# Window attention and a gated expert layer on one core: a visit's values moved ahead of its scores, and operand sums spread over 48 steps

## The chip, the cores and the metric

The kernel runs on one core of a Trainium2 chip. The metric is device time in microseconds (us) from start to end of one execution. Three executions of the kernel before took 1054.36, 1054.43 and 1058.17 us; the median is 1054.43. TensorE is called PE here, its weight loads PEld, VectorE DVE, ScalarE ACT, GpSimd POOL, and the DMA queue of SyncE SP.

## The reference

```python
# q, k, v: (8 batches, 8 heads, 576 positions, 64)
scores = q @ k^T / 8, masked to the 64 positions up to the query's own
attn   = softmax(scores) @ v
x      = attn as (4608 tokens, 512)
xn     = x / sqrt(mean(x*x) + 1e-6) * rms_g
out    = (silu(xn @ w_gate) * (xn @ w_val)) @ w_out     # 512 -> 1536 -> 512
```

## The kernel before

**Tiles and steps.** The 4608 tokens are nine tiles of 512 (t = 0 to 8). A tile's expert layer is 32 steps: 24 steps produce the 1536 hidden values (`expert_in`, from tile 3 on `expert_in_7`), 8 produce the output (`expert_out`); up to tile 2 both accumulate in the three banks of the pool `ps_mo`. Each step begins with `tick()`, which calls `advance` (L1105): it takes from a list called `plan`, sorted by step number, every piece of work whose step has come. Step 0 is the first of tile 0, step 32 the first of tile 1, and so on. From tile 1, chunk 3 (step 44) on, `group()` (L63) puts each group of PE instructions behind the PE instruction that was traced last before it, so PE runs the groups in the order of the program. Inside a group, and on ACT, DVE, POOL and SP, a list scheduler with a timeline of its own chooses the order before the kernel runs; each engine then executes its list in that fixed order and waits at its head.

**Attention.** Batches 2 to 7 are handled pair of heads by pair of heads, numbered n = 8 to 31, in visits. Visit n stands at step `visit_at(n)` (L613): 27, 32, 37, 42.5, 47.5, and then every 8 steps, so in a tile from the third on visits fall at steps 7.5, 15.5, 23.5 and 31.5. A visit (L618) computes the scores of pair n (`scores_of_pair`, L404) and the attention values of pair n-2 (`attention_values`, L498). The scores of blocks 1 to 8 go to two banks of PSUM named `sc` (32 small matmuls), those of block 0 to the last columns of a third bank (4 small matmuls, called `x` in the trace). The values' first part (g = 0, 20 matmuls) goes to the first 320 columns of this same bank `x`, the second part (g = 1, 16 matmuls) to a bank `xp`. Both come from the pool `ps_x`, which has two banks. DVE masks the scores block by block (L399, block 0 first), ACT takes exponentials (L402), DVE reciprocals (L428); POOL multiplies and moves the weights (`move`, L371, 16 instructions for a pair), DVE transposes them (`turn`, L374), and two visits later PE multiplies them with v. ACT copies the values out of the two banks (L564), squares them (L570); the squares are added up over the pairs (L575, POOL or DVE).

**Normalising.** At steps 25 and 27 of a tile the batch's sums of squares become roots (matmul `tot`, L700, into a bank of `ps_x`; then DVE L688 to L695), DVE scales x (L740), and from tile 3 on `combine` (L762) forms sums and differences on DVE (L779, L780, L782, L785) and casts them on ACT (L773) and POOL (L774).

**Operand sums.** From tile 3 on the hidden layer uses seven products of half-size blocks in place of eight. The sums of weights that this needs are made by `prepare` (L856), 24 pieces: for each of six chunks c, four steps. A piece is 8, 4, 4 or 8 PE matmuls with a signed unit matrix into one bank called `chain` (pool `ps_mi`, one bank), a cast on ACT (L890, tile `hl`), a subtraction on DVE (L891) that reads the same bank, and two DMAs to DRAM (L893). The next piece writes the same bank, so its first matmul waits for the subtraction. The pieces stand at step `PREP0 + (PREP1 - PREP0) * j / 24`, j = 0 to 23.

Of the kernel before, what the change touches and what calls it, by code (L numbers as in the profile page):

```python
# [26 lines left out]
B, H, S, D = 8, 8, 576, 64  # L27
# [9 lines left out]
XSPLIT = 320  # L37
# [5 lines left out]
MOVES = (8.7, 7, 4.5, 4)  # L43
FIRST7 = 3
ORDERED = (1, 3)
PREP0, PREP1 = 32.2, 55.5
ST = 2 * NBLK * P - D
NRB = 2
S1, LK1, LV1, LQ1 = [-2, 1, 3, 6, 10, 12.5, 15.5, 19], 2.5, 6, 7
# [7 lines left out]
def tile_window_attention_moe(  # L57
# [34 lines left out]
    def x_bank(name):  # L92
        return ps_x.tile([P, TT], F32, tag="xp", name=name)
# [262 lines left out]
    def big(n):  # L356

        t = wk.tile([P, ST], I32, tag="st8", name=f"pm_{n}", bufs=NST).bitcast(F32)
        return (t[:, a : a + NBLK * P].rearrange("p (j k) -> p j k", k=P) for a in (0, ST - NBLK * P))

    def slot(u):

        return (u - 1) % NBLK
# [15 lines left out]
    def units(g, h):  # L379
        return [1 + 4 * g + 2 * h + i for i in range(2)] + ([0] if g == h == 0 else [])  # L380

    def quarter(out, qt, kk, h, j):

        halves = kk.rearrange("p (n c) -> p n c", c=D)
        hd = slice(h * D, (h + 1) * D)
        nc.tensor.matmul(  # L386
            out.rearrange("p (n c) -> p n c", c=D),
            lhsT=qt[hd, j * D : (j + 1) * D],
            rhs=halves[hd, :1, :] if j == 0 else halves[hd, j : j - 2 : -1, :] if j % 2 == 0 else halves[hd, j - 1 : j + 1, :],
            start=True,  # L390
            stop=True,
            skip_group_check=True,
        )
# [3 lines left out]
    def masked(out, sc, mask, low):  # L397

        nc.vector.tensor_tensor_reduce(out, sc, mask, -QK_SCALE, 3.0e38, ALU.add, ALU.min, low)  # L399

    def weigh(part, low, total):
        nc.scalar.activation(part, part, AF.Exp, bias=low, scale=-1.0, accum_out=total)  # L402

    def scores_of_pair(n, qk, first):  # L404

        qt, kk = qk
        sc = [
            pool.tile([P, TT], F32, tag=tag, name=f"sc_{n}_{h}").rearrange("p (i k) -> p i k", k=P)
            for h, (pool, tag) in enumerate(((ps_sc, "sc"), (ps_tr, "tr")))
        ]  # L410
        for h in range(2):
            quarter(first[h * D : (h + 1) * D, :D], qt, kk, h, 0)
        for i in range(4):
            for h, par in QUARTERS:
                quarter(sc[h][par * D : (par + 1) * D, i, :], qt, kk, h, 2 * i + 1 + par)
        p, m = big(n)
        st = wk.tile([P, 3, NBLK], F32, tag="st", name=f"st_{n}", bufs=3)
        order = [0] + [u for h in range(2) for u in units(0, h) + units(1, h) if u]
        place = {u: sc[h][:, 2 * g + i, :] for g in range(2) for h in range(2) for i, u in enumerate(units(g, h)) if u}
        for u in order:  # L420
            w, v = P if u else D, slot(u)
            masked(p[:, v, :w], place[u] if u else first[:, :D], blocked[:, :P] if u else blocked[:, P:],
                   st[:, 0, v : v + 1])
        for u in order:
            w, v = P if u else D, slot(u)
            weigh(p[:, v, :w], st[:, 0, v : v + 1], st[:, 1, v : v + 1])
        nc.vector.tensor_scalar(st[:, 1, :], st[:, 1, :], 1e-9, None, ALU.add)
        nc.vector.reciprocal(st[:, 2, :], st[:, 1, :])  # L428
        whole[n] = p, m, st[:, 2, :]
# [87 lines left out]
    def attention(b):  # L517
# [12 lines left out]
        def score(hp, g, first=None):  # L530
            qk = qs[hp], pairs[hp][0]
            if b < TB:
                soft[hp, g] = scores(b * NPAIR + hp, g, qk)
            elif g == 0:
                scores_of_pair(b * NPAIR + hp, qk, first)
# [75 lines left out]
    visits = {}  # L611
# [4 lines left out]
        return VISITS[n] if n < 4 else VISITS[4] + 8 * (n - 4)  # L616

    def visit(n):  # L618

        xp = x_bank(f"x0_{n}")  # L620
        if n in visits:
            visits[n][0](xp[:, XSPLIT:])
        if n - 2 in visits:
            visits[n - 2][1](0, xp)
            visits[n - 2][1](1)

    def first_batch():
        load_queries, load_keys, score, to_keys, values, roots, normal, moved, turned = attention(0)
# [430 lines left out]
    for n in range(NPAIR * TB, NPAIR * B + 2):  # L1059
        at_step(visit_at(n), partial(visit, n))  # L1060
# [117 lines left out]
```

## Time and profile before

| what | value |
|---|---|
| median of three executions | 1054.43 us |
| profiled execution | 1057.74 us, span of its instructions 1056.0 us |
| PE busy | 987.1 us (93%) |
| DVE, POOL, ACT busy | 626.5, 520.6, 510.0 us |
| granted clock of PE, mean of the span | 0.976 |

The span is from the first instruction's start to the last one's end. "Busy" is the union of an engine's instructions. A wait row names the instruction that stood at the head of its engine's queue and the instruction whose end released it. [...]

### The profile page before, as it was taken

To read this page: it belongs to the slowest core of one execution; us is meant where nothing else is said; L and a number is where in the kernel's file an instruction comes from. 1 tells how busy PE (TensorE), PEld (TensorE's weight loads), DVE (VectorE), ACT (ScalarE), POOL (GpSimd) and SP (SyncE) were. 2 spreads that over 40 slices of the span, in tenths; PEclk is the share of its full clock that TensorE was granted. 3 is DMA by queue.
4 is the path that set the end of the run, shared out by engine and by line. 5 is a ranking of instruction groups with operands and counts; after the bars stand their busy time and mean duration, and the time that the engine had idled before them with its cause. 6 is when DMAs were issued, how large, how long until landed. Compare 5 with 4: busy or idle time off the path is not lost.

```text
span 1056.0 us, 20885 instructions
## 1 busy us (share of the span) xinstructions
PE 987.1 (93%) x7883; PEld 645.8 (61%) x7895; DVE 626.5 (59%) x1655; ACT 510.0 (48%) x1303; POOL 520.6 (49%) x667
## 2 busy tenths in 40 slices
PE   7789987998899999989998999999989999999998
PEld 5544544454454445468846884688458847856875
DVE  5688857424457434856695669566856574531550
ACT  5557867235342434246535663565356524522531
POOL 3325635808256666756766575657575314200210
PEclk9889988999899999999999999899999999999999
DMA  7647853024231334147724672376235605632501
GB/s 282 196 155 217 263 174 91 31 62 139 72 114 56 115 116 136 64 123 231 219 69 141 216 216 68 116 231 212 72 102 180 180 33 144 206 110 83 157 2 40
DMA packets 81317, 143.45 MB, mean 136 GB/s; under 512 B 25792, under 2 KB 38336, under 8 KB 81216
## 3 DMA queue, kind: packets, MB, share of 16 engines
q1 hardware_dynamic: 80640, 140.93, 43.5%
q8 instruction: 62, 1.02, 0.4%
q10 hardware_dynamic: 576, 1.18, 0.3%
q14 instruction: 39, 0.32, 0.1%
HBM read 121.64 MB, written 20.45 MB: 135 GB/s over the span
## 4 chain that ended last, share of the span: by engine, by line
PE 53%; DVE 19%; POOL 13%; ACT 9%; issue 3%; DMA 2%; SPq 0%; DVEq 0%; POOLq 0%; ACTq 0%
PE bk L922 19%; POOL pm L371 12%; ACT pm L402 4%; PE bk L790 3%; PE bk L791 3%; PE bk L792 3%; DVE xb L740 3%; PE pv L790 2%; PE pg L790 2%; PE pv L792 2%; PE pg L791 2%; PE pv L791 2%; PE pg L792 2%; PE sc L386 2%; DVE pm L374 2%
## 5 line engine op out<-in xcount | busy, mean ns | idle before, releaser
L922 PEld LDWEIGHTS <-wt 128*128 128x128 f16 x3024 | 294.8, 98 | 48.1 <-issue 12.2
L371 POOL TENSOR_TENSOR pm<-pm,st 32x288 f32<-32x288 f32 (+1 forms) x384 | 262.8, 684 | 99.2 <-DVE st L428 38.6
L922 PE MATMUL bk<-xn,wt 128*128 128x256 f16 x1728 | 207.9, 273 | 10.6 <-DVE th L954 6.3
L959 POOL TENSOR_TENSOR h<-th,h 128x512 f16<-128x512 f32 x60 | 69.3, 1159 | 167.6 <-ACT h L958 147.3
L922 PE MATMUL bk<-wt,wt 128*128 128x256 f16 x1224 | 150.4, 273 | 0.0
L790 PE MATMUL bk<-wt,h 128*128 128x512 f16 (+1 forms) x300 | 112.5, 375 | 0.0
L791 PE MATMUL bk<-wt,h 128*128 128x512 f16 (+1 forms) x300 | 112.4, 375 | 0.0
L792 PE MATMUL bk<-wt,h 128*128 128x512 f16 (+1 forms) x300 | 112.4, 375 | 0.0
L402 ACT ACTIVATE pm<-pm,st 128x128 f32<-128x128 f32 (+1 forms) x216 | 83.7, 392 | 9.1 <-DVE st L399 9.0
L952 ACT ACTIVATE th<-bk,hsc 128x256 f32<-128x256 f32 x108 | 51.4, 476 | 63.3 <-DVE bk L981 30.4
L792 PEld LDWEIGHTS <-h 128*128 128x128 f16 x436 | 43.1, 99 | 51.7 <-issue 4.4
L790 PEld LDWEIGHTS <-h 128*128 128x128 f16 x436 | 43.3, 99 | 48.8 <-issue 2.9
L791 PEld LDWEIGHTS <-h 128*128 128x128 f16 x436 | 43.1, 99 | 49.1 <-issue 3.3
L978 DVE TENSOR_TENSOR bk<-bk,s 128x512 f32<-128x512 f32 x36 | 25.0, 695 | 75.8 <-PE bk L922 70.3
L953 DVE SCALAR_TENSOR_TENSOR th<-th,bk 128x256 f32<-128x256 f32 x108 | 44.9, 416 | 36.2 <-ACT th L952 36.2
L386 PE MATMUL sc<-kv,q 64*64 64x128 f32 (+1 forms) x1056 | 56.6, 295 | 8.5 <-DMA q<-q 4.8
L773 ACT CAST xn<-xb 128x192 f16<-128x192 f32 (+7 forms) x33 | 13.0, 424 | 101.8 <-DVE xb L740 101.7
L374 DVE STREAM_TRANSPOSE pm<-pm 128x1024 f32<-128x1024 f32 x24 | 29.8, 1242 | 49.8 <-POOL pm L371 49.8
L958 ACT CAST h<-th 128x512 f16<-128x512 f32 x72 | 44.5, 618 | 29.7 <-DVE th L954 28.5
L790 PE MATMUL pv<-xn,wt 128*128 128x512 f16 x144 | 56.6, 393 | 1.8 <-DVE th L839 1.8
L790 PE MATMUL pg<-xn,wt 128*128 128x512 f16 x144 | 55.2, 383 | 2.1 <-ACT wt L235 1.8
L791 PE MATMUL pv<-xn,wt 128*128 128x512 f16 x144 | 56.2, 390 | 0.1
(189 smaller groups left out, 1902.7 us busy)
## 6 DMA issues: line engine op xcount, KB each, us to landing
wt<-sevens SPq DMA_DIRECT2D x108, 512.0 KB, 4.3
kv<-kv SPq DMA_DIRECT2D x28, 608.0 KB, 4.8
wt<-sevens SPq DMA_DIRECT2D x36, 256.0 KB, 3.2
q<-q SPq DMA_DIRECT2D x28, 288.0 KB, 3.4
kv<-kv SPq DMA_DIRECT2D x56, 128.0 KB, 4.8
out<-ot SPq DMA_DIRECT2D x27, 256.0 KB, 2.0
st<-w_gate SPq DMA_DIRECT2D x6, 1024.0 KB, 6.7
st<-w_val SPq DMA_DIRECT2D x6, 1024.0 KB, 6.0
```

The lines of the kernel that those rows point to most:

```text
L371: nc.gpsimd.tensor_tensor(m[to, :us, fr], p[fr, :us, to], r, ALU.mult)
L374: nc.vector.transpose(p[:, : NBLK - 1, :], m[:, : NBLK - 1, :])
L386: nc.tensor.matmul(out.rearrange("p (n c) -> p n c", c=D), lhsT=qt[hd, j * D : (j + 1) * D], rhs=halves[hd, :1, :] if j == 0 else halves[h ...
L402: nc.scalar.activation(part, part, AF.Exp, bias=low, scale=-1.0, accum_out=total)
L790: nc.tensor.matmul(acc, lhsT=lh, rhs=rh, start=first, stop=False)
L791: nc.tensor.matmul(acc, lhsT=lh, rhs=rl, start=False, stop=False)
L792: nc.tensor.matmul(acc, lhsT=ll, rhs=rh, start=False, stop=last)
L922: nc.tensor.matmul(acc[:, i * HT : (i + 1) * HT], lhsT=w[:, i, l, kt, :], rhs=b[:, m, kt, :], start=at_start, stop=kt == 1 and j == 2, ski ...
L952: nc.scalar.activation(cols, acc[:, :HT], AF.Tanh, scale=th_scale[:, c : c + 1])
L953: nc.vector.scalar_tensor_tensor(cols, cols, 1.0, acc[:, :HT], ALU.add, ALU.mult)
L958: nc.scalar.copy(hh, th)
L959: (nc.vector if t and c == NC - 1 else nc.gpsimd).tensor_tensor(hl, th, hh, ALU.subtract)
```

## The change

The constant `PREP1` goes from 55.5 to 80: the 24 pieces of `prepare` stand 2 steps apart (steps 32.2 to 78) in place of 1 step. In a visit the values of pair n-2 come first, in two banks of their own; then the scores of pair n, blocks 1 to 8 first and block 0 last, in a third bank taken from the same pool of two. DVE masks block 0 last, and ACT takes its exponential last.

```diff
-PREP0, PREP1 = 32.2, 55.5
+PREP0, PREP1 = 32.2, 80
@@ scores_of_pair
-        for h in range(2):
-            quarter(first[h * D : (h + 1) * D, :D], qt, kk, h, 0)
         for i in range(4):
             for h, par in QUARTERS:
                 quarter(sc[h][par * D : (par + 1) * D, i, :], qt, kk, h, 2 * i + 1 + par)
+        for h in range(2):
+            quarter(first[h * D : (h + 1) * D, :D], qt, kk, h, 0)
...
-        order = [0] + [u for h in range(2) for u in units(0, h) + units(1, h) if u]
+        order = [u for h in range(2) for u in units(0, h) + units(1, h) if u] + [0]
@@ visit
-
-        xp = x_bank(f"x0_{n}")
+        if n - 2 in visits:
+            for g in range(2):
+                visits[n - 2][1](g)
         if n in visits:
-            visits[n][0](xp[:, XSPLIT:])
-        if n - 2 in visits:
-            visits[n - 2][1](0, xp)
-            visits[n - 2][1](1)
+            visits[n][0](x_bank(f"x0_{n}"))
```

## Rows read from the trace of the kernel before

**Rows 1.** The page's busy times: engine, us (share of the span) x instructions.

```profile
PE 987.1 (93%) x7883; PEld 645.8 (61%) x7895; DVE 626.5 (59%) x1655; ACT 510.0 (48%) x1303; POOL 520.6 (49%) x667
```

**Rows 2.** Waits of PE: waiting line <- releaser: us in total, times, longest us.

```profile
PE x L507 <- DVE st L399: 13.2, 8, 3.1
PE chain L881 <- DVE hl L891: 6.8, 3, 4.4
PE bk L922 <- DVE th L954: 6.3, 4, 1.6
...
PE chain L888 <- DVE hl L891: 4.3, 4, 1.5
...
PE tot L700 <- DVE ssq L575: 1.4, 3, 0.6
```

**Rows 3.** Windows, cold clock: stretch, its us, busy us (instructions) by engine, granted clock, DMA.

```profile
264.88:271.70 6.82, 4.73 (x16) 2.25 (x16) 3.98 (x6) 1.10 (x2) 2.23 (x2) 0.50 0.20 60
667.65:674.48 6.83, 6.31 (x46) 3.57 (x47) 2.54 (x21) 5.83 (x24) 3.76 (x5) 0.50 0.73 233
```

**Rows 4.** Windows over the first and last step-31.5 visit with a wait, each whole.

```profile
452.57:458.46 5.89, 3.53 (x74) 3.05 (x73) 4.86 (x23) 4.82 (x17) 5.21 (x7) 0.79 0.26 90
771.71:777.80 6.09, 2.94 (x73) 2.52 (x73) 5.75 (x22) 4.41 (x13) 6.09 (x6) 0.92 0.16 45
```

**Rows 5.** Timeline of PE, DVE and ACT in these visits: start us, us, ..., [idle <-releaser].

```profile
456.14 1.53 PE L507 MATMUL x<-pm,kv 64*64 64x64 f32 x20 [2.36 <-DVE st L399]
...
456.63 0.40 ACT L773 CAST xn<-t 128x256 f16<-128x256 f32 x1
...
771.87 1.04 PE L386 MATMUL sc<-kv,q 64*64 64x128 f32 x30
776.06 0.95 PE L507 MATMUL x<-pm,kv 64*64 64x64 f32 x20 [3.15 <-DVE st L399]
...
774.58 1.28 DVE L785 TENSOR_TENSOR t<-xb,t 128x448 f32<-128x448 f32 x1
...
776.14 0.56 ACT L773 CAST xn<-t 128x448 f16<-128x448 f32 x1
778.49 0.41 ACT L564 COPY xb<-x 128x320 f32<-128x320 f32 x1
```

**Rows 6.** Timeline of the last visit, which has values and no scores.

```profile
842.74 0.95 PE L507 MATMUL x<-pm,kv 64*64 64x64 f32 x20
843.74 0.43 ACT L564 COPY xb<-x 128x320 f32<-128x320 f32 x1 [0.92 <-PE x L507]
844.09 1.16 PE L922 MATMUL bk<-xn,wt 128*128 128x256 f16 x9
```

**Rows 7.** Timeline of a step-23.5 visit.

```profile
526.29 0.56 PE L507 MATMUL xp<-pm,kv 128*64 128x64 f32 x10
527.69 0.51 ACT L952 ACTIVATE th<-wt,hsc 128x256 f32<-128x256 f32 x1 [1.15 <-DVE wt L985]
527.79 0.95 PE L507 MATMUL x<-pm,kv 64*64 64x64 f32 x20 [0.94 <-DVE st L399]
```

**Rows 8.** Timeline from a step-7.5 visit's weights to the PE wait behind them.

```profile
487.49 1.48 POOL L575 TENSOR_TENSOR ssq<-ssq,kv 128x576 f32<-128x576 f32 x1 [3.54 <-DVE st L428]
488.93 11.48 POOL L371 TENSOR_TENSOR pm<-pm,st 32x288 f32<-32x288 f32 x16
...
502.56 1.47 PE L922 MATMUL bk<-xn,wt 128*128 128x256 f16 x12 [1.58 <-DVE th L954]
```

**Rows 9.** Timeline of the longest wait between two pieces of `prepare`.

```profile
264.76 1.25 DVE L374 STREAM_TRANSPOSE pm<-pm 128x1024 f32<-128x1024 f32 x1 [6.66 <-POOL pm L371]
...
266.85 0.66 DVE L839 SCALAR_TENSOR_TENSOR th<-th,pg 128x512 f32<-128x512 f32 x1
...
266.97 0.37 PE L881 MATMUL chain<-wt,unit 128*128 128x256 f16 x1 [4.45 <-DVE hl L891]
```

**Rows 10.** The page's costliest groups: exponentials: count | busy us, mean ns | idle before.

```profile
L402 ACT ACTIVATE pm<-pm,st 128x128 f32<-128x128 f32 (+1 forms) x216 | 83.7, 392 | 9.1 <-DVE st L399 9.0
```

## The prediction

> **What bounds the kernel now.** I read the page's busy times first: PE is busy for 987.1 us, 93% of the span [rows 1]. From tile 1 on PE runs its groups in the order of the program, so time can only come from PE's waits, from its cold clock, or from work added to it. Second came the waits of PE [rows 2]. Two lines of that list belong to the two halves of the change. The values (L507) wait 13.2 us in 8 places for DVE's mask of block 0: they write the bank that DVE is still reading. The matmuls of `prepare` wait for the subtraction of the piece before: 6.8 us at L881 and 4.3 us at L888, together 11.1 us in 7 places. The other lines of the list are not touched by the edit directly. [...] Last I read the places themselves in order of time [rows 4 to 9], to see what is late next when a wait goes.
>
> **Visits, step 31.5.** The 13.2 us split by place: a step-23.5 visit waits 0.94 [rows 7], three times, 2.8 together; so the step-31.5 visits have 10.4, nearly all of it in four, from 2.36 in the first to 3.15 in the last [rows 5]. There DVE finishes `combine` (L785, ends 775.86) 4.15 us after PE began the visit at 771.71, and masks block 0 only then. After the change the values no longer wait, but block 0's scores need a bank, and the pool has two: the one they get is that of the values' first part, free when ACT has copied it (L564). So the question is where ACT's list has this copy. The last cast of `combine` stands ahead of the exponentials today [rows 5], belongs to an earlier step, and hangs on L785. DVE's list has L785 ahead of block 0's mask; the mask could start some 0.3 us after the visit's first matmul, so the scheduler believed L785 to be done about then, and its cast ready before the values' 20 matmuls (1.00 us until the copy, [rows 6]) let the copy start. I therefore take the cast first, the copy behind it. Then in the first visit the cast ends at 457.03, 4.46 after the start at 452.57; plus the copy, 0.41, plus block 0's four matmuls, some 0.3 by L386's rows: the visit takes 5.2 where it took 5.89 [rows 4]. In the last: 776.70 is 4.99 after the start, so 5.7 where it took 6.09. Gains 0.7 and 0.4; for all four I take 0.4 each, **1.6 us**. Bounds: -0.2 each, if the two that are not shown lose as much as the copy exceeds the mask (0.41 against 0.21); and all 10.4 plus the cold clock, if the copy comes first (a rival below). PE's wait is then for ACT, about as long as before, so the cold windows behind it stay.
>
> What the row shows [rows 5] is that ACT, though it could have copied, casts and exponentiates in list order, and that its list had the cast first. [...]
>
> **Visits, step 23.5 (three).** Here the list puts ten matmuls of `xp` ahead of the values on `x` [rows 7], so the scheduler saw block 0's mask come late, behind L985, and the cast-like hyperbolic tangent on `wt` (527.69), which hangs on L985, later than the new copy can start. I take the copy first: nothing holds block 0, **2.8 us** gained. If the tangent comes first, it ends at 528.20, the copy at 528.6, and block 0 waits 1.2 (it is due 2.25 after the start at 525.15: 1.35 of values [rows 6] and some 0.9 of scores, whose 1.2 in [rows 5] includes the last one's drain): a loss of 0.8 in three visits.
>
> **Visits, the others.** In an ordinary visit the copy can start after 1.00 us and takes 0.43 [rows 6], block 0 is due at 2.25: no wait. The values cost PE the same before or after the scores. With copies and squares ahead of the exponentials, the addition of squares on POOL (1.48 us) [rows 8] need not stand between the reciprocal and the moves any more; but the exponentials start 1.35 us later, since the scores come behind the values. Ordinary visits at steps 7.5 and 15.5 feed the chain scores, exponentials, moves (11.48), transpose, and behind that a PE wait of 1.58 [rows 8], which occurs four times [rows 2]. Net 0.1 earlier by these rows at least, 1.48 at best if the exponentials fill the time; loss at most 1.35 each if the scheduler leaves the addition last. I take 0.25 each, **1.0 us**, bounds -5.4 and +5.9. The wait of the `tot` matmul for the sum of squares, 1.4 us in three places [rows 2], goes, because copies and squares no longer stand behind exponentials: **1.4 us**.
>
> **`prepare`.** Its matmuls, 24 casts and 24 subtractions stay; so do its DMAs, on SP's queue, which PE does not wait for in any row of its waits. With two steps between pieces six of the seven waits, 11.1 less 4.45, have the 12 matmuls of one more step to hide in, and the largest of them is about 1.5 [rows 2]: **6.6 us** gained. The seventh, 4.45 us, is another matter [rows 9]: DVE stood for 6.66 us at a transpose that waits for POOL's moves, and the subtraction behind it was only the first of the late ones. The hidden layer's own DVE work stands behind the same transpose, and PE has three accumulation banks, two of them used per pair of steps. So I keep the 4.45 and the cold clock behind it [rows 3]; bounds: gone with its clock, 4.45 + 2.4 = 6.9 better; or longer, since PE now arrives earlier at a chain that POOL sets. Twelve pieces move behind step 55.5, four into the output steps of tile 1 and eight into tile 2. Each brings a cast and a subtraction to ACT and DVE and a bank that PE waits for. Today's mean wait is 11.1/24 = 0.46; at that mean twelve cost 5.5, at best nothing. I take **1.0 us** of loss, near the lower end, as the pieces lie twice as far apart.
>
> **Sum.** 1.6 + 2.8 + 1.0 + 1.4 + 6.6 - 1.0 = 12.4 us. From the profiled execution's 1057.74 that is 1045.3; that execution lies 3.3 above the median 1054.43 and inside the runs shown (up to 1058.17), and the result will be a median, so I predict 1054.4 - 12.4 = **1042.0**.
>
> **Rivals.**
> A, the wait is really gone: the copy stands ahead of the last cast in the step-31.5 visits. The 10.4 go instead of 1.6, and with them the cold windows behind them; one of these is shown, and half of 6.31 is 3.2 [rows 3]. 12.4 + 8.8 + 3.2 = 24.4: 1030.0. For it: the scheduler's margin is a fraction of a microsecond either way. Against it: the cast belongs to an earlier step, and DVE's list order. Chance 0.17.
> B, PE only arrives earlier at the same POOL moves: tile 1's gain of 6.6 turns into longer waits behind transposes. Already 6.66 us of idle DVE stand at one such place [rows 9]. 12.4 - 6.6 = 5.8: 1048.6; with the chain of [rows 8] late as well, 1051. Against it: the transposes of the later pairs lie two visits ahead of their use, and POOL was idle between. Chance 0.24.
> C, slower: ACT's list keeps exponentials ahead of the copy. They don't need block 0, so nothing forbids it, and today the copy starts 1.8 us after the last cast's end, with exponentials between [rows 5]. Their masks wait for the scores of blocks 1 to 8, done when block 0 is due; so one exponential ahead makes block 0, and PE behind it, wait for a mask (0.21), the exponential (0.39, [rows 10]) and the copy (0.43), 1.03 us in each of 20 visits from tile 1's middle on: 20.6, less 12.4, slower by 8.2: 1062.6. It decides from about 0.6 us a visit. Against it: the copy is the earlier piece of the program and ready first. Chance 0.15.
> The forecast itself has the rest, 0.44, its own range 1036 to 1048.
>
> **How the numbers follow.** Range: from just below A's 1030 up to where B ends and C begins, 1056; C is left out, and what may lie beyond A. About 0.5% (5.3 us) is what a measurement of this kernel can tell from no change, so faster means under 1049.1, slower over 1059.7. Faster: 0.93 of the forecast's 0.44, all of A, a third of B: 0.66. Slower: nearly all of C, 0.14. Same: 0.20.
>
> **What would show it.** Right: in the waits of PE, no L507 behind L399; in its place L386 on `x` behind ACT's copy L564 in step-31.5 visits, 2 to 3 us each, and none in ordinary visits; the lines of `prepare` nearly empty, but one wait of about 4 us in tile 1 behind a DVE transpose, perhaps under the name of the hidden layer; the granted clock still at 0.5 after the step-31.5 visits. Wrong: no wait at L386 at all (A), waits of PE for L839, L840 or L954 that grow by as much as those of `prepare` shrink (B), or L386 waiting in most of the 20 visits (C). The prediction also fails if the scheduler's lists change far from the edit, in tile 0 say, which no row here can tell.

## The result, and the profile after

The changed kernel takes 1046.49 us in the median of four runs (1044.36 to 1047.02), the kernel before 1055.13 beside it (1054.36 to 1058.17): a ratio of 0.9909, 95% interval 0.9884 to 0.9934, so 9.6 us by the ratio (8.6 between the medians). The prediction had 1042.0 and 12.4 us. A second measurement of the same kernel, in the experiments below, gives 0.9918 (0.9903 to 0.9933), 8.7 us. The profiled execution took 1044.36, its span 1042.6, against 1057.74 and 1056.0 before. The first is the shortest of the four runs after and the second lies near the longest before, so the spans are 13.4 us apart, more than the medians.

The page's busy times of the changed kernel (engine, us, share of the span, instructions), against [rows 1]: PE is busy for 5.0 us less with as many matmuls, at nearly the same granted clock (a mean of 0.975 of full speed against 0.976). Part of it is the new order itself, which the prediction took to cost PE the same: from tile 3 on an ordinary visit took 2.74 us (from 586.26 to 589.01) and takes 2.48 (from 576.00 to 578.48), while in tile 2 one took 2.33 and takes 2.48. The rest of the 13.4 us by which the span is shorter, 8.4, is time in which PE stood idle, most of it in the waits below.

```profile
PE 982.1 (94%) x7883; PEld 643.7 (62%) x7895; DVE 621.3 (60%) x1655; ACT 511.2 (49%) x1303; POOL 517.8 (50%) x667
```

The waits of PE in the changed kernel, against [rows 2] (waiting line <- releaser: us in total, times, longest; the lines of the code have moved up by two):

```profile
PE x L386 <- ACT xb L564: 15.5, 4, 4.9
PE chain L879 <- DVE hl L889: 6.0, 2, 5.7
...
PE bk L920 <- DVE th L952: 3.6, 4, 0.9
PE bk L920 <- DVE wt L983: 2.2, 2, 1.1
```

The 13.2 us of the values behind the mask of block 0 are gone, and so are the 1.4 us of the `tot` matmul. In their place block 0's scores wait for ACT's copy L564, four times, 15.5 us: the mechanism that was forecast, but half as long again as the 10.2 us that it replaces (13.2 less the three step-23.5 visits and 0.2 in tile 2). The 11.1 us of `prepare` are 6.0, nearly all in one place. The wait behind the hidden layer's L954 (now L952) fell from 6.3 to 3.6.

Windows over the first and the last step-31.5 visit, against [rows 4] (stretch, its us, busy us and instructions of PE, PEld, DVE, ACT, POOL, granted clock, DMA share, GB/s):

```profile
441.93:446.97 5.04, 2.71 (x73) 2.27 (x73) 4.64 (x21) 4.00 (x11) 5.03 (x7) 1.00 0.13 46
756.49:764.24 7.75, 2.85 (x73) 2.36 (x73) 7.36 (x21) 5.20 (x11) 7.75 (x6) 0.87 0.11 31
```

The first became shorter (5.89 before), the last longer (6.09 before). The timeline of the last one says why (start us, us, engine, line, operation, tiles, and in brackets the idle time before it and its releaser), against [rows 5]:

```profile
756.49 1.41 PE L507 MATMUL xp<-pm,kv 64*64 64x64 f32 x36
757.83 1.10 PE L386 MATMUL sc<-kv,q 64*64 64x128 f32 x32
...
761.16 1.27 DVE L783 TENSOR_TENSOR t<-xb,t 128x448 f32<-128x448 f32 x1
761.56 1.26 ACT L1001 ACTIVATE ot<-bk,hsc 128x512 f32<-128x512 f32 x2
...
762.71 0.56 ACT L771 CAST xn<-t 128x448 f16<-128x448 f32 x1
...
763.35 0.70 ACT L564 COPY xb<-xp 128x320 f32<-128x320 f32 x2
...
763.83 0.48 PE L386 MATMUL x<-kv,q 64*64 64x64 f32 x4 [4.90 <-ACT xb L564]
```

PE is through with the values and the scores of blocks 1 to 8 2.44 us after the visit began. The last subtraction of `combine` on DVE (L783) ends only at 762.43, 5.94 after the beginning; its cast and the copy follow on ACT, and block 0's scores start at 763.83. Before, the same subtraction ended 4.15 after the visit's first matmul.

### The profile page after: what moved, and what is told of

Its sections match the earlier page's. It is cut to its first block, busy times and chain, and to the rows that moved or that the text cites. A ratio compares the mean times of both kernels' runs of the same rounds, so it can differ in the third digit from the quotient of the medians.

```text
span 1042.6 us, 20888 instructions
## 1 busy us (share of the span) xinstructions
PE 982.1 (94%) x7883; PEld 643.7 (62%) x7895; DVE 621.3 (60%) x1655; ACT 511.2 (49%) x1303; POOL 517.8 (50%) x667
## 4 chain that ended last, share of the span: by engine, by line
PE 56%; DVE 16%; POOL 15%; ACT 8%; issue 3%; DMA 1%; SPq 0%; POOLq 0%; DVEq 0%; ACTq 0%
PE bk L920 20%; POOL pm L371 14%; ACT pm L402 5%; PE bk L788 4%; PE bk L789 4%; PE bk L790 4%; PE xp L507 3%; PE sc L386 3%; PE pg L788 2%; DVE xb L738 2%; PE pg L789 2%; PE pg L790 2%; PE pv L788 2%; PE pv L789 2%; PE pv L790 2%
## 5 line engine op out<-in xcount | busy, mean ns | idle before, releaser
L788 PE MATMUL bk<-wt,h 128*128 128x512 f16 (+1 forms) x300 | 114.2, 381 | 0.0
L789 PE MATMUL bk<-wt,h 128*128 128x512 f16 (+1 forms) x300 | 114.2, 381 | 0.0
L790 PE MATMUL bk<-wt,h 128*128 128x512 f16 (+1 forms) x300 | 113.8, 379 | 0.0
L790 PEld LDWEIGHTS <-h 128*128 128x128 f16 x436 | 43.7, 100 | 51.6 <-issue 5.4
L771 ACT CAST xn<-xb 128x192 f16<-128x192 f32 (+7 forms) x33 | 12.9, 422 | 102.9 <-DVE xb L738 102.7
L386 PE MATMUL sc<-kv,q 64*64 64x128 f32 (+1 forms) x1056 | 54.7, 296 | 8.8 <-DMA q<-q 5.1
L788 PE MATMUL pv<-xn,wt 128*128 128x512 f16 x144 | 55.4, 384 | 1.9 <-DVE th L837 1.9
L789 PE MATMUL pv<-xn,wt 128*128 128x512 f16 x144 | 55.3, 384 | 0.1
L772 POOL TENSOR_TENSOR xn<-xb,xn 128x192 f16<-128x192 f32 (+7 forms) x33 | 28.7, 892 | 53.6 <-ACT xn L771 53.2
```

Of the source, the lines that this page charges most:

```text
L386: nc.tensor.matmul(out.rearrange("p (n c) -> p n c", c=D), lhsT=qt[hd, j * D : (j + 1) * D], rhs=halves[hd, :1, :] if j == 0 else halves[h ...
L788: nc.tensor.matmul(acc, lhsT=lh, rhs=rh, start=first, stop=False)
L789: nc.tensor.matmul(acc, lhsT=lh, rhs=rl, start=False, stop=False)
L790: nc.tensor.matmul(acc, lhsT=ll, rhs=rh, start=False, stop=last)
```

## The experiments

Times are medians, each beside runs of the kernel before on the same chip (1053.72, 1055.24 and 1054.39 us in the three series); a ratio is to these, with its 95% interval. The three series ran on three chips, so kernels of different series are best compared by their ratios. The four kernels of the first series answer where the gain comes from, and what sets the time at a step-31.5 visit.

**Each half alone.**

```
prep_only, against the kernel before:
-PREP0, PREP1 = 32.2, 55.5
+PREP0, PREP1 = 32.2, 80
visit_only, against the changed kernel:
-PREP0, PREP1 = 32.2, 80
+PREP0, PREP1 = 32.2, 55.5
```

> The kernel before with only the end of `prepare` moved from step 55.5 to step 80; the visits stay as they were. Theory 1 (nearly all of the gain is `prepare`'s; what the visits gain inside a tile is given back at the next step-31.5 visit, where DVE's chain through the last subtraction of `combine` sets the time): 0.991 to 0.994 of the time before, 1046 to 1049 us, that is within 3 us of the changed kernel. Theory 2 (both halves count as the prediction had it: prepare 5.6 of 12.4, visits and what hangs on them 6.8): about 0.995, 1049 to 1051 us. In the trace both expect the waits of `prepare` (11.1 us) down to about 6 in one or two places and the 13 us of the values behind the mask of block 0 as they were.

> The changed kernel with `prepare` ending at step 55.5 again: only the order inside a visit is changed. Theory 1: 0.998 to 1.000 of the time before, 1053 to 1055 us; the four step-31.5 visits show PE waiting 14 to 16 us for the copy of the values' first part, the three step-23.5 visits none, and the time from one step-31.5 visit to the next is 105 us as before. Theory 2: 0.993 to 0.995, 1047 to 1050 us, with the waits of the step-31.5 visits at 10 us or less. Both keep some 11 us of PE waits in `prepare`.

Measured: `prepare` alone 1050.99, ratio 0.9981 (0.9967 to 0.9994), 2.0 us; the visits alone 1053.12, ratio 0.9995 (0.9983 to 1.0007). The second is what theory 1 said; the first, by the ratio, is what neither said: the halves are worth about 2.6 us apart and 8.7 to 9.6 together. The waits of PE with `prepare` alone (this profile is of the longest of its twelve executions, 1055.89 us):

```profile
PE x L507 <- DVE st L399: 16.6, 9, 3.1
...
PE chain L881 <- DVE hl L891: 5.3, 1, 5.3
```

and two of the visits in tile 1 in its timeline (DVE's transpose, the mask of block 0 behind it, PE's values):

```profile
251.59 0.95 PE L507 MATMUL x<-pm,kv 64*64 64x64 f32 x20 [1.42 <-DVE st L399]
...
269.62 1.25 DVE L374 STREAM_TRANSPOSE pm<-pm 128x1024 f32<-128x1024 f32 x1 [3.36 <-POOL pm L371]
270.79 0.18 DVE L399 CUSTOM_DVE_ANT_0 pm<-x,blocked 128x64 f32<-128x64 f32 x1
...
271.04 1.53 PE L507 MATMUL x<-pm,kv 64*64 64x64 f32 x20 [2.28 <-DVE st L399]
```

This is the place of [rows 9] again. DVE stands at a transpose that waits for POOL's moves; before the change a subtraction of `prepare` was behind it, here it is the mask of block 0, and PE's values wait for that, at 1.42 and 2.28 us where there was no such wait before. With the visits alone it is the other way round. Its waits of PE:

```profile
PE x L386 <- ACT xb L564: 16.2, 5, 4.9
PE chain L879 <- DVE hl L889: 6.1, 2, 3.1
...
PE chain L886 <- DVE hl L889: 3.6, 3, 1.5
```

The mask is out of PE's way, and `prepare` still waits 9.7 us in five places.

**The same normalisation, one step earlier.**

```
norm_early, against the changed kernel, in the call that plans the later batches:
-        for h, part in attention_events(b, -2, 2, (3, 6, 7, 25, 27)):
+        for h, part in attention_events(b, -2, 2, (3, 6, 7, 24, 26)):
```

> The changed kernel with both halves of the normalisation (roots of the mean square, products, `combine`) one step earlier, at steps 24 and 26 instead of 25 and 27; nothing else. Theory 1: the chain on DVE from the mean square to the last subtraction of `combine` decides when the first copy of a step-31.5 visit can start, so a step (3.3 us) earlier takes some 3 us off each of the four waits of 2.3 to 4.9 us: 15.5 us of waits fall to 3 to 6, the cold clock behind some of them goes, and the time falls by 9 to 13 us, to 1034 to 1038. Theory 2 (DVE and ACT have no room in this stretch; the sum of squares of the step-23.5 visit, or POOL, comes late, not the step at which the chain is issued): the matmul of the mean square waits 3 us for the sum of squares instead, and the time stays within 3 us of the changed kernel.

Measured: 1038.50, ratio 0.9858 (0.9838 to 0.9877). Its waits of PE:

```profile
PE chain L886 <- DVE hl L889: 10.2, 1, 10.2
PE x L386 <- ACT xb L564: 5.2, 4, 1.6
...
PE tot L698 <- DVE ssq L575: 3.3, 4, 1.3
```

The time is 0.5 us above the range of theory 1. 15.5 us became 5.2, as theory 1 said: when DVE ends `combine` decides when PE gets its bank. Theory 2's wait at the sum of squares is there too, but at 3.3 us in all. What the prediction of this run missed is in tile 1: the one wait of `prepare` grew from 5.7 to 10.2.

**The visit itself, one step later.**

```
visit_late, against the changed kernel, in visit_at:
-        return VISITS[n] if n < 4 else VISITS[4] + 8 * (n - 4)
+        return VISITS[n] if n < 4 else VISITS[4] + 8 * (n - 4) + (n % 4 == 2)
```

> The changed kernel with every step-31.5 visit from tile 2 on (and the one at the end of tile 1) one step later, at step 0.5 of the next tile; its transposes and the loads of its queries and keys move with it, nothing else. Theory 1: by then the last cast of `combine` is done, the copy starts at once, and 13 to 16 us of waits go with their cold clock: 1028 to 1034. Theory 2 (the time is only handed on, PE reaches the next stretch earlier and waits there for DVE's masks, the hyperbolic tangents or the operands of the next tile): 1041 to 1046 with the waits under other lines.

Measured: 1031.15, ratio 0.9785 (0.9767 to 0.9804), in the middle of what theory 1 gave. By the code the edit also moves POOL's moves of the visit's own pair by a step, which the expectation leaves out. Its waits of PE:

```profile
PE bk L920 <- DVE th L952: 5.2, 4, 1.3
PE x L386 <- ACT xb L564: 5.1, 7, 1.6
...
PE bk L920 <- ACT wt L941: 1.6, 3, 0.5
```

One window over the same stretch of the later tiles, first of the changed kernel, then with late visits:

```profile
455.00:775.00 320.00, 304.11 (x2850) 223.52 (x2849) 221.18 (x586) 166.75 (x470) 207.80 (x275) 0.97 0.51 157
```

```profile
455.00:775.00 320.00, 309.71 (x3001) 232.07 (x3002) 231.71 (x605) 170.77 (x484) 218.93 (x288) 1.00 0.52 166
```

Some of the time does turn up elsewhere, as theory 2 has it (the hidden layer's wait is 1.6 us longer, that for L941 is new), but the granted clock of these 320 us is 1.00 instead of 0.97, and 151 more of PE's matmuls lie in them. The gap stood before a bank and before `xb`, which has one buffer; no buffer was added, and a step's delay took most of it away (15.5 us became 5.1).

**Once more, and the new order in the first tiles only.**

```
mix_early, against the changed kernel:
+NEW_UNTIL = 15
 (scores_of_pair)  block 0 last if n < NEW_UNTIL, else first, as before
 (visit)           values, then scores if n < NEW_UNTIL, else scores, then values, as before
```

> The changed kernel once more, beside the two halves' chip. The halves alone gave 0.9981 (`prepare`) and 0.9995 (visits) of the time before, 2.6 us together; if the halves are worth no more together than apart, this gives 0.997 to 0.998 (1050 to 1052 us) and the first measurement was drift; if they need each other, 0.990 to 0.992 (1044 to 1047 us) again.

> `prepare` to step 80 as changed; the new order inside a visit only for the visits up to step 63.5 (those of tile 0 and tile 1), the old order from step 71.5 on. Theory 3 (the halves need each other in tile 1: there DVE is late with both the subtractions of `prepare` and the mask of block 0, and either one alone leaves PE waiting at the other): nearly the whole gain, 0.991 to 0.994, 1045 to 1048 us, with no wait of the values for the mask before 350 us, but again 0.9 us in each step-23.5 visit and 2 to 3 us in each step-31.5 visit. Rival: the gain that needs both lies in the steady tiles; then 0.997 to 0.999 as with `prepare` alone, 1050 to 1053 us.

Measured: the changed kernel 1045.71 again, 0.9918 (0.9903 to 0.9933), on another chip than the halves, so the ratios are what compares; the halves do need each other. With the new order up to step 63.5 alone 1048.10, 0.9939 (0.9926 to 0.9953): 6.4 us by the ratio, of 8.7 in the same series, come with the visits of the first two tiles and `prepare` together; the new order in all the later tiles is worth the rest, 2.4 us between the medians. The waits of PE in that mixed kernel (its line numbers are up to 14 higher than those of the changed kernel):

```profile
PE x L513 <- DVE st L400: 12.8, 7, 3.1
PE bk L934 <- DVE th L966: 6.2, 4, 1.6
PE chain L893 <- DVE hl L903: 6.0, 2, 5.7
...
PE tot L712 <- DVE ssq L581: 1.3, 3, 0.4
```

The later tiles wait as before, and `prepare` as after. The first values that wait for the mask do so at 446.92 us, as theory 3 said.

**The wait that `prepare` kept.** In the changed kernel it stands here (ACT, DVE and PE at the end of tile 1):

```profile
321.27 0.35 ACT L771 CAST xn<-xb 128x192 f16<-128x192 f32 x1 [6.48 <-DVE xb L738]
...
323.79 0.35 ACT L771 CAST wt<-t 128x192 f16<-128x192 f32 x1
...
324.62 0.57 ACT L888 CAST hl<-chain 128x512 f16<-128x512 f32 x1
...
325.23 0.69 DVE L889 TENSOR_TENSOR hl<-chain,hl 128x512 f16<-128x512 f32 x1 [0.86 <-ACT hl L888]
...
325.98 0.37 PE L879 MATMUL chain<-wt,unit 128*128 128x256 f16 x1 [5.71 <-DVE hl L889]
```

The cast of the piece stands on ACT behind casts of `combine` (L771), which hang on DVE's normalisation of the next batch (L738). `prepare` reaches the output steps of tile 1 only since it runs to step 80.

```
prep_gap, against the changed kernel:
-        at_step(PREP0 + (PREP1 - PREP0) * j / (4 * NC), partial(prepare, j // 4, j % 4))
+        at_step(32.2 + 2 * j if j < 12 else 64.2 + 2 * (j - 12), partial(prepare, j // 4, j % 4))
```

> The changed kernel with the pieces of `prepare` kept out of the output steps of tile 1: twelve at every second step from 32.2 to 54.2, twelve from 64.2 to 86.2. Theory: the one long wait left in `prepare` (5.7 us at 320 us, then the clock at 0.5 for 3.4 us) comes because a subtraction of `prepare` stands on DVE behind the normalisation of the next batch at steps 57 and 59; without pieces there it goes, 4 to 7 us faster than the changed kernel, 1039 to 1043 us. Rival: PE arrives earlier at the normalisation itself or at the hidden layer's work on DVE and waits there as long; 1045 to 1047 us, the 5.7 us under another line between 300 and 345 us.

Measured: 1039.85, ratio 0.9861 (0.9848 to 0.9875), 5.9 us under the changed kernel in the same series, as the theory said. Of the waits in `prepare` 0.3 us are left:

```profile
PE chain L879 <- DVE hl L889: 0.3, 1, 0.3
```

**Moves together.** late_norm has the edits of visit_late and norm_early, late_gap those of visit_late and prep_gap, late_norm_gap all three; late_old_order is mix_early with the edit of visit_late.

> The changed kernel with both moves together: the step-31.5 visits one step later and the normalisation one step earlier. Each alone measured 1031.2 and 1038.5 us. If both act on the same wait (the copy of the values' first part behind the end of `combine`), the second adds only what the first left, 0.8 to 1.6 us in three places, less 0.7 us of waiting for the sum of squares in each tile that an earlier normalisation brought: 1029 to 1032 us. If they act on different waits, their gains add up: 1022 to 1025 us.

Measured: 1035.52, ratio 0.9820 (0.9807 to 0.9834), outside both ranges: 4.4 us above late visits alone (3.7 by the ratios). Its waits of PE:

```profile
PE chain L886 <- DVE hl L889: 10.2, 1, 10.2
...
PE tot L698 <- DVE ssq L575: 3.5, 4, 1.3
...
PE x L386 <- ACT xb L564: 1.2, 4, 0.3
```

At the visits the two edits do act on the same wait (5.1 us became 1.2), but the sum of squares takes 3.5 of that, and the earlier normalisation makes the wait of `prepare` in tile 1 10.2 us where visit_late has 5.7: 4.1 us lost in all, about what was measured.

> The changed kernel with the step-31.5 visits one step later and the pieces of `prepare` kept out of the output steps of tile 1. Alone these measured 1031.2 and 1039.9 us, 14.5 and 5.9 us below the changed kernel. They act on different waits (the copy behind `combine` in tiles 2 to 6; the subtraction of `prepare` behind the normalisation in tile 1), so the gains add up: 1024 to 1027 us. Rival (one of them has what the other took, as with the normalisation one step earlier, where late_norm came out 4 us above late alone): 1030 to 1033.

> The same with the normalisation one step earlier as well. Without the gap this combination had one wait of 10.2 us in `prepare` at 313 us and the clock at 0.5 for 10.2 us behind it; without pieces in the output steps both are gone, some 15 us off the 1035.5 measured without the gap: 1019 to 1022 us. Rival: the early normalisation only moves the wait to the sum of squares and the hidden layer; 1025 to 1028, no better than late_gap.

Measured: 1022.58, ratio 0.9707 (0.9693 to 0.9720), for late_gap, the fastest together with late_norm_gap at 1023.19, 0.9704 (0.9690 to 0.9717). The two edits of late_gap add up and a little more, 1.4 us below the range: different waits. late_norm_gap lies between its two ranges. The gap took 12.3 us off late_norm and not some 15: of the stretch at 0.50 there, from about 317.8 to 328.1, only the last 4.4 us lie behind the wait, which ends at 323.7. With the gap the early normalisation no longer hurts, and does not help either: the waits of L386 fall from 4.5 to 1.2 us, and 3.2 us at the sum of squares come instead.

> The kernel with the step-31.5 visits one step later, but the old order inside a visit from step 71.5 on (new order up to step 64.5, `prepare` to step 80). It stands to the kernel with late visits (1031.2 us) as the one with the new order only up to step 63.5 (1048.1) stands to the changed kernel (1045.7, 2.4 us faster). Theory (what the new order gains inside a steady tile is given back at the step-31.5 visit only because PE waits there for the end of `combine`): with that wait gone the new order is worth its full price there: 2.8 us at step-23.5 visits, 1.4 us at the sum of squares, 0.65 us of the wait behind the hidden layer four times, some 7 us in all: 1036 to 1040 us. Rival (the new order is worth 2.4 us wherever the step-31.5 visit stands): 1033 to 1034.5.

Measured: 1033.20, ratio 0.9807 (0.9792 to 0.9822), against 0.9785 with the new order throughout, on another chip and with overlapping intervals. The theory failed, the rival held: the new order is worth about 2 us in the later tiles, there too. The waits of the old order with late visits:

```profile
PE bk L934 <- DVE th L966: 11.6, 8, 1.6
...
PE x L513 <- DVE st L400: 2.7, 3, 0.9
```

Against these, visit_late has 10.4 us less (6.4 behind the hidden layer, 2.7 at the mask, 1.3 at the sum of squares) and 6.7 more (5.1 before the copy, 1.6 for L941). So about two thirds of what the new order saves in waits in the later tiles it spends at other places. Once the visits come late, the step-31.5 visits of the old order do not wait for the mask at all (three places are left, the step-23.5 ones), while three of the four of the new order still wait for the copy, 0.8 to 1.6 us each.

## Why the prediction was right in the sum and not in its terms

**Step 31.5, forecast 1.6 us gained: wrong in size and sign.** The mechanism held: ACT has the last cast ahead of the copy, the wait has moved from the mask to L564, and the clock is still at 0.50 behind visits (from 764.00 to 767.40, say). But the working took the end of L785 after the visit's first matmul as given, 4.15 us, although the other terms were to bring PE there earlier. The four visits, from their first matmul to the first one behind them, and PE's time from the end of one to the start of the next, in us:

| step-31.5 visit | way to it, before | after | visit, before | after |
|---|---|---|---|---|
| first | | | 5.89 | 5.04 |
| second | 100.73 | 98.61 | 4.64 | 7.08 |
| third | 100.57 | 98.31 | 6.09 | 6.94 |
| fourth | 101.22 | 98.58 | 6.09 | 7.75 |

Ahead of the first visit PE saves nothing (33.2 us from the step-23.5 visit's start before, 33.3 after), and there the forecast of 5.2 us was close. On the way to the other three it saves 7.0 us, and the visits give 5.0 of them back. All four together lose 4.1 us where 1.6 were to be gained.

Before the third of the four visits the chain on DVE is seen whole. Before (DVE's first operation of the roots, the last of `combine`, and PE's values behind the mask):

```profile
640.87 0.34 DVE L688 TENSOR_SCALAR r<-tot 128x192 f32<-128x192 f32 x1
...
666.89 1.08 DVE L785 TENSOR_TENSOR t<-xb,t 128x384 f32<-128x384 f32 x1
...
668.17 0.37 PE L507 MATMUL x<-pm,kv 64*64 64x64 f32 x2 [2.56 <-DVE st L399]
```

After (PE's step-23.5 visit, the same two of DVE, PE's scores of block 0):

```profile
618.91 1.41 PE L507 MATMUL xp<-pm,kv 64*64 64x64 f32 x36
...
628.72 0.35 DVE L686 TENSOR_SCALAR r<-tot 128x192 f32<-128x192 f32 x1
...
655.12 1.08 DVE L783 TENSOR_TENSOR t<-xb,t 128x384 f32<-128x384 f32 x1
...
657.50 0.48 PE L386 MATMUL x<-kv,q 64*64 64x64 f32 x4 [4.09 <-ACT xb L564]
```

From the first to the last of these operations DVE takes 27.1 us before and 27.5 after, and it starts 10.5 and 9.8 us behind PE's step-23.5 visit (630.37 and 618.91). So PE goes on 37.8 us after that visit before, 38.6 after, whatever PE saved in between. PE was ready for it after 35.2 before and 34.5 after. It arrives 0.7 earlier. Behind the end of `combine` come 1.3 us of ACT (the end of L1001, the cast, the copy) where 0.2 of a mask came, and DVE, which ends 0.3 earlier, makes up little of that: the wait grows by 1.5. Over the four visits 10.2 us of waits became 15.5. norm_early and visit_late show that it is this chain: move it or PE's need by a step, and 10 us of waits go.

**Step 23.5, 2.8 us, and `tot`, 1.4: right in place.** Both waits are gone, and with the shorter order the three visits take 2.48 us each where they took 3.75, 3.8 less in all. **Ordinary visits, 1.0: right in sign.** The wait behind L954 fell from 1.58 to 0.90 each, 2.7 us in all. But all this, save the last of the L954 waits, lies between one step-31.5 visit and the next, and there 5.0 of 7.0 us are given back. What stays, 2.1, and the 0.9 gained in the first visit are of the size of the 2.4 us between mix_early and the changed kernel. The prediction gave the later tiles 6.8.

**`prepare`, 6.6 less 1.0: about right in sum, wrong in kind.** The waits fell by 5.1 us, one long one stays and a cold clock with it, as forecast (0.50 from 325.28 to 328.69 us). But it is not the one of [rows 9], which is gone; it belongs to the pieces that were moved into the output steps of tile 1. The price of 1.0 for the moved pieces was too low: keeping them out of these steps brings 5.9. And the gain is not `prepare`'s alone. The prediction priced the halves apart and added them; in tile 1 they are two works behind the same transposes on DVE, and PE waits for whichever is left (4.45 us for a subtraction of `prepare` before, 2.28 for the mask with `prepare` alone). That is 2.0 us for `prepare` alone, about nothing for the visits alone, and 6.4 for both up to step 63.5. The half of PE's busy time that the prediction counts for a cold clock (2.4 and 3.2 us) stands in the trace of the kernel before: at a granted clock of 0.50 the matmuls of L790 to L792, 512 columns each, started 0.43 us apart (from 670.89 to 674.30), at 1.00 0.22 (from 674.83 to 676.12).

**The rivals.** A did not come: the copy stands behind the last cast. From the code it hardly could have saved more than half a microsecond a visit: the copy writes `xb`, of which there is one buffer, and L783 and POOL's L772 read it. In the four visits L772's last reading of `xb` ends 0.03 to 0.45 us before the copy starts. The working should have seen that, and with it that the order of ACT's list is not the only thing that can hold the copy; no run tells the two apart. A second buffer was not tried. A's price was real, though: with the wait nearly out of the way, visit_late gains 14.5 us. B, PE arriving earlier at the same work, came true, but on DVE's normalisation in the later tiles instead of POOL's moves in tile 1. C did not: block 0 waits in four visits of the 20.

So 1042.0 came near 1046.5 in part by luck: a loss of 4.1 at step 31.5, where 1.6 were to be gained, stood against gains that were set too low in tile 1 (5.6 against 6.4), behind L954 (1.0 against 2.7) and at step 23.5 (2.8 against 3.8). The range held, the working only in part.

## What to carry to other kernels

When a wait is removed from an engine that runs in order, ask from which event the next release is counted. If a chain on another engine sets it (here 27 us on DVE between two visits), time saved inside that stretch comes back as a longer wait at its end (here 5.0 of 7.0 us), and what brought the gain here was moving the chain or the need for it by a step (15.5 us of waits became 5.2 and 5.1). Two waits behind the same held instruction are one wait with two names: price them together, for either edit alone may bring next to nothing (here 2.0 us and about nothing, against 8.7 to 9.6 together). And look at what a spread piece of work lands beside: 24 pieces at a wider pace were good (together with the visits), those that fell into the normalisation's steps cost 5.9 us.

## What the runs showed of the hardware

In the changed kernel DVE's steps of the root took longer beside POOL's work than after it. POOL works on L746 from 313.35 to 317.88:

```profile
313.35 4.53 POOL L746 TENSOR_TENSOR xn<-xb,xn 128x384 f16<-128x384 f32 x4 [3.12 <-ACT xn L744]
...
315.17 0.95 DVE L691 TENSOR_TENSOR r<-r 128x192 f32<-128x192 f32 x1
...
318.13 0.36 DVE L691 TENSOR_TENSOR r<-r 128x192 f32<-128x192 f32 x1
```

This step of the root (L691, on 192 columns) takes 0.95 us beside it and 0.36 once it is done. In the later tiles the steps of the root take about 0.7 on 192 columns beside POOL's moves, longer than the 0.56 that 384 columns take when POOL is idle (it does nothing in the 6.96 us before 651.01):

```profile
628.20 11.83 POOL L371 TENSOR_TENSOR pm<-pm,st 32x288 f32<-32x288 f32 x16 [7.82 <-ACT h L956]
630.30 0.71 DVE L692 SCALAR_TENSOR_TENSOR r<-r,r 128x192 f32<-128x192 f32 x1
645.09 0.56 DVE L693 SCALAR_TENSOR_TENSOR r<-r,r 128x384 f32<-128x384 f32 x1
```

So part of the 27 us of DVE's chain fell beside POOL's work, at 0.65 to 0.78 us a step; how much time it would save to keep them apart was not tried.
